# Batch 0 taken whole: both halves' attention from the lead-in's scores, and one output stage by seven block products

## The chip, the cores and the metric

The kernel runs on one core of a Trainium2 chip. The metric is the time of one execution on the device in microseconds. All numbers of the profile come from one profiled execution of the kernel.

## What is computed

For 4 batches of 8 heads, 768 positions and head size 64, each query attends to its neighbours closer than 16 positions and to 24 blocks of 32 keys, each represented by the maximum of its keys and the mean of its values (the block score has log 32 added). The result goes through a two-layer feed-forward network.

```python
k_sum = k.reshape(B, H, nb, block, D).max(axis=3)
v_sum = v.reshape(B, H, nb, block, D).mean(axis=3)
scores_l = np.where(mask_l, scale * q @ k.T, -1e9)      # mask_l: |i - j| < 16
scores_s = scale * q @ k_sum.T + np.log(block)
a = softmax(np.concatenate([scores_l, scores_s], axis=-1))
x = a @ np.concatenate([v, v_sum])                       # then [3072, 512]
h = x @ w_in                                             # 512 -> 2048
out = (h * sigmoid(1.702 * h)) @ w_out                   # 2048 -> 512
```

## The kernel before

The program is written as one long sequence; every engine executes its instructions in the order in which they are written, and each waits for the data that it needs. Work is placed beside other work by hand: small dictionaries (`plan0`, `plan1`, `plan`, `todo`) say which attention step is written after which slot of a matrix product.

A batch is 768 tokens in two halves of 384 (`HALF`), each of three tiles of 128. Heads go in four pairs `p`. The hidden layer has 16 tiles `nt` of 128; for a half and an `nt` it is four matmuls of 128x128 weights with 384 columns into PSUM (`ph`), then a gelu on ACT into `gT`.

**Two ways of attention.** In the lead-in, batch 0's first half goes by tiles of 128 queries against their own 128 keys (`s_own`), with small products for the 32 positions across a tile's edge (`s_edges`), the mask being added in PSUM by a matmul of a prepared `bias` (`s_bias`); `s_exp` takes the exponential. The block scores are products of their own (`b_turn`, `b_exp`), and values come from `v0n`, the batch's values as loaded, and `vs4`, its block sums (`v_sum`, `v_copy`), by `av_own`, `av_edges` and `av_blocks`; `v_norm` divides. All other half batches go by tiles of 64 queries against 128 rows that hold 64 own keys, two halos of 16 and the 24 block maxima with the rest (`kx`, filled by `tk` or `xk`, `rest_k`, `key_halos`, `key_rows`): `scores`, `mask`, `values`. For those the values' rows are laid out the same way in `vw`: `value_rows` has the halos copied by SP, sums blocks on PE (`vsum`), adds on DVE (`block_sums`) and has the sums' rows copied by SP (`sum_dmas`).

**Two ways of output.** Batch 0 takes its halves one after the other, and each half's output is 48 plain matmuls of 512 columns (`ff_out`, accumulated in `po`). Batches 1 to 3 take both halves together: from `gT`, DVE makes four sums `gs` (`g_sums`), from w_out once four sums `ws` (`w_sum`), and the output of both halves is made from seven block products (`product`, numbers 1 to 7, for each of three tiles `t`), each eight matmuls of 256 columns, accumulated in `poA`, `poB` and `poC`, in the order of `seq`.

**The order around the change.** Lead-in (scores and values of batch 0, first half, 874 to 983); hidden layer of that half (1061 to 1065); its output with batch 0's second half of attention beside it (`plan0`, 1072 to 1077); hidden layer of the second half with batch 1's keys and half its queries turned (`todo`, 1079 to 1087); its output with the rest of batch 1's attention beside it (`plan1`, 1090 to 1096); then the loop over batches 1 and 2 (1100), in which the hidden layer of both halves is followed by seven products with the next batch's whole attention beside them (`plan`), and batch 3 at the end with other means.

**Queues.** POOL issues the loads that cast from float32: k, q, v, w_in, w_out in the order of lines 876 to 895, then `load_batch`. SP issues the copies inside the chip's memory, the transposes by DMA (`xk`, `xq`, `dx`) and the output's stores.

**Buffers.** In PSUM after the lead-in, `pmm` has four banks (hidden tiles, `po`), `psb` two buffers of two banks (turns, scores and others).

Of the kernel before, what the change touches and what calls it, by code (L numbers as in the profile page):

```python
# [35 lines left out]
def kernel(  # L36
# [55 lines left out]
    def load_q0(g):  # L92
        if g == 0:
            qb2["early"] = castp2.tile([128, H, JH, D], BF16, name="qb", tag="qb")
        pool.dma_start(out=qb2["early"][:, 4 * g:4 * g + 4].rearrange("p h r d -> p h (r d)"),
                       in_=q[0, 4 * g:4 * g + 4, 0:HALF].rearrange("h (p r) d -> p h (r d)", r=JH))

    def load_q1(a):
        if a == 0:
            qb2["late"] = castp2.tile([128, H, JH, D], BF16, name="qb", tag="qb")  # L100
        pool.dma_start(out=qb2["late"][:, 2 * a:2 * a + 2].rearrange("p h r d -> p h (r d)"),
                       in_=q[0, 2 * a:2 * a + 2, HALF:S].rearrange("h (p r) d -> p h (r d)", r=JH))
# [29 lines left out]
    warm = lead.tile([128, 512], BF16, name="warm")  # L132
    band = [lead.tile([128, 128 + 2 * PAD], BF16, name=f"band{i}") for i in range(2)]
    NE = HALF + JH * 32
    bias = lead.tile([128, NE], BF16, name="bias")

# [13 lines left out]
    def bands():  # L150

        n = 128 + 2 * PAD
        src, step = wide, 1
        for dst in (band[0], band[1], band[0], band[1]):
            n -= step
            dve.tensor_tensor(out=dst[:, 0:n], in0=src[:, 0:n], in1=src[:, step:step + n], op=ALU.max)
            src, step = dst, 2 * step
        n -= 15
        dve.tensor_tensor(out=band[0][:, 0:n], in0=band[1][:, 0:n], in1=band[1][:, 15:15 + n], op=ALU.max)
        dve.tensor_scalar(out=band[1][:, 1:1 + n], in0=band[0][:, 0:n], scalar1=-FAR, scalar2=FAR,  # L160
                          op0=ALU.mult, op1=ALU.add)
        near, edge = (bias[:, a:b].rearrange("p (j c) -> p j c", j=JH) for a, b in ((0, HALF), (HALF, NE)))
        dve.memset(edge, FAR)
        for o, r, c in ((near, slice(0, 128), slice(34, 162)), (edge, slice(0, 32), slice(2, 34)),
                        (edge, slice(96, 128), slice(162, 194))):
            dve.tensor_copy(out=o[r], in_=band[1][r, c].unsqueeze(1)
                            .to_broadcast([r.stop - r.start, JH, c.stop - c.start]))

# [39 lines left out]
    w_out_sb = keep.tile([128, NT, d_model], F16, name="w_out_sb")  # L208

# [21 lines left out]
    def load_batch(b):  # L231
        if b == 3:
            pool.tensor_copy(out=gate2, in_=qTs[0][:, 0, 0:1])
        load_turned(k, b, kb2, "kb")
# [5 lines left out]
        if b < 3:  # L240
            load_turned(q, b, qb2, "qb", (1,) if b == 1 else (0, 1))
# [23 lines left out]
    def vsum(s):  # L265

        if s == 1 and not vs_ps[0]:
            ps = [pmm.tile([128, 512], F32, name="ps_vs", tag="mm") for e in range(2)]
        else:
            big = psb.tile([128, 1024], F32, name="ps_vs", tag="big")  # L270
            ps = [big[:, 0:512], big[:, 512:1024]]
# [44 lines left out]

    def vrows0():

        dve.tensor_copy(out=gate3[:, 1:2], in_=gate3[:, 0:1])
        v6 = vs4.rearrange("p (a g) c -> p g a c", g=4)  # L320
        o6 = vs.rearrange("p (a g) c -> p g a c", g=4)
        for g in range(4):
            dve.tensor_copy(out=o6[0:nb, g, :, 0:D], in_=v6[32 * g:32 * g + nb, g, :, 0:D])
        w5 = vw[0].rearrange("p (j e) h c -> p j e h c", e=2)
        sum_dmas(w5, JH)
# [53 lines left out]
    def k_late(p, eng):  # L379

        k4 = kx[p][0].rearrange("p (j e) c -> p j e c", e=2)
        for e in range(2):
            eng.tensor_copy(out=k4[:, JH - 1:NJ, e, e * 64:e * 64 + 64],
                            in_=kn[:, p, HALF - 128:S].rearrange("p (j e c) -> p j e c", e=2, c=64)[:, :, e])

    def q_turn(p):
# [3 lines left out]
        turn_plain(st["Q", p], qb2["early"][:, 2 * p:2 * p + 2])  # L390

    def q_copy(p, eng):
        copy(eng, qT[p][0][:, 0:HALF].rearrange("p (c r) -> p c r", r=JH),
# [8 lines left out]
    def q_late(p, eng):  # L402
        if p != 2:
            ps = psb.tile([128, 2048], BF16, name="ps_q", tag="big")
        else:
            ps = pmm.tile([128, 1024], BF16, name="ps_q", tag="mm")
        turn_plain(ps[:, 0:HALF], qb2["late"][:, 2 * p:2 * p + 2])
        copy(eng, qT[p][0][:, HALF:S].rearrange("p (c r) -> p c r", r=JH),
             ps[:, 0:HALF].rearrange("p (r c) -> p c r", r=JH))

    def s_bias(p):

        big = st["S", p] = pbig.tile([128, 1024], F32, name="ps_s", tag="big")
# [4 lines left out]
    def s_own(p):  # L418

        big = st["S", p]  # L420
        for j in range(JH):
            for h in range(2):
                r, o = slice(h * 64, h * 64 + 64), slice(j * 128, j * 128 + 128)
                pe.matmul(out=big[:, h * 512 + j * 128:h * 512 + j * 128 + 128], lhsT=kn[r, p, o],
                          rhs=qTs[0][r, p, o], start=False, stop=True, skip_group_check=True)

    def s_edges(p):

        big = st["S", p]
        for j in range(JH):  # L430
            for h in range(2):
                r, o = slice(h * 64, h * 64 + 64), h * 512 + HALF + j * 32
                pe.matmul(out=big[0:32, o:o + 32], lhsT=kn[r, p, j * 128 + 128:j * 128 + 160],
                          rhs=qTs[0][r, p, j * 128 + 96:j * 128 + 128], start=False, stop=True,
                          skip_group_check=True)
                if j:
                    pe.matmul(out=big[96:128, o:o + 32], lhsT=kn[r, p, j * 128 - 32:j * 128],
                              rhs=qTs[0][r, p, j * 128:j * 128 + 32], start=False, stop=True,
                              skip_group_check=True)

    def s_exp(p):
        a = a_sb[p] = lead.tile([128, 2, NE], BF16, name="a_sb", tag="a_sb", bufs=4)
        act.activation(out=a, in_=st["S", p].rearrange("p (h c) -> p h c", h=2)[:, :, 0:NE],
                       func=ACT.Exp, scale=scale)

    def b_turn(g):

        st["B", g] = pturn.tile([128, 512], F32, name="ps_b", tag="turn")
        for i in range(2):
            for h in range(2):  # L450
                o = i * 64 + h * 32
                r = slice(h * 64, h * 64 + 64)
                pe.matmul(out=st["B", g][o:o + 32, 0:HALF], lhsT=ks0[r, 2 * g + i],
                          rhs=qT[2 * g + i][0][r, 0:HALF], start=True, stop=True, skip_group_check=True)

    def b_exp(g):
        ab = st["ab", g] = lead.tile([128, HALF], BF16, name="ab", tag="ab", bufs=2)
        act.activation(out=ab, in_=st["B", g][:, 0:HALF], func=ACT.Exp, scale=scale)
# [32 lines left out]
    def av_own(p):  # L491

        if p < 2:
            st["V", p] = pturn.tile([128, 512], F32, name="ps_av", tag="turn")
        else:
            st["V", p] = pbig.tile([128, 1024], F32, name="ps_av", tag="big")[:, 0:512]
        pv, a = pv_of(p), a_sb[p]
        for hh in range(2):
            for j in range(JH):
                pe.matmul(out=pv[:, hh, j, 0:D + 1], lhsT=a[:, hh, j * 128:j * 128 + 128],  # L500
                          rhs=v0n[:, 2 * p + hh, j, 0:D + 1],
                          start=(hh == 0 and j == 0), stop=False, skip_group_check=True)

    def av_edges(p):
        pv = pv_of(p)
        for hh in range(2):
            ah = a_sb[p][:, hh]
            for j in range(JH):
                o = HALF + j * 32
                pe.matmul(out=pv[96:128, hh, j, 0:D + 1], lhsT=ah[0:32, o:o + 32],  # L510
                          rhs=v0n[0:32, 2 * p + hh, j + 1, 0:D + 1],
                          start=False, stop=False, skip_group_check=True)
                if j:
                    pe.matmul(out=pv[0:32, hh, j, 0:D + 1], lhsT=ah[96:128, o:o + 32],
                              rhs=v0n[96:128, 2 * p + hh, j - 1, 0:D + 1],
                              start=False, stop=False, skip_group_check=True)

    def av_blocks(p):
        for j in range(JH):
            pe.matmul(out=pv_of(p)[:, :, j, :],  # L520
                      lhsT=st["ab", p // 2][:, j * 128:(j + 1) * 128],
# [25 lines left out]
    def tq(p, s, eng):  # L547
        ps = pmm.tile([128, 1024], BF16, name="ps_t", tag="mm")[:, 0:S]
# [37 lines left out]
    def values(b, half, g):  # L586

        if b == 1:
            banks = [pmm.tile([128, 512], F32, name="ps_av", tag="mm") for i in range(2)]
        else:  # L590
            ps = psb.tile([128, 1024], F32, name="ps_av", tag="big")
            banks = [ps[:, i * 512:i * 512 + 512] for i in range(2)]
        pvs = []
        for i in range(2):
# [4 lines left out]
            for hh in range(2):  # L599
                for j in range(JH):  # L600
                    for e in range(2):
                        t = 2 * j + e
                        pe.matmul(out=pv[e * 64:e * 64 + 64, hh, j, :], lhsT=a[:, hh, t, :],
                                  rhs=vw[b % 2][:, half * TH + t, p + hh * NP if b else 2 * p + hh, 0:D + 1],
                                  start=True, stop=True, skip_group_check=True)
        x2[g] = attp.tile([128, 2, JH, 2, D], F16, name="x2", tag="x2", bufs=4)
        for i in range(2):
            norm(x2[g][:, :, :, i].rearrange("p h j d -> p j h d") if b else x2[g][:, i], pvs[i])
# [59 lines left out]
    def g_sums(j, eng=dve, which=(0, 1, 2, 3)):  # L668

        a1, a2 = gTb[:, j], gTb[:, j + NT // 2]  # L670
        l, r = slice(0, HALF), slice(HALF, S)
        for w in which:
            a, b_, op = {0: (a1[:, r], a2[:, r], ALU.add), 1: (gs[:, 0, j], a1[:, l], ALU.subtract),
                         2: (a1[:, l], a1[:, r], ALU.subtract), 3: (a2[:, l], gs[:, 1, j], ALU.subtract)}[w]
            eng.tensor_tensor(out=gs[:, w, j], in0=a, in1=b_, op=op)
# [84 lines left out]
    def product(b, t, what):  # L760
# [23 lines left out]
        def keep_it(name):  # L784
            if b + 1 == B and name == "s1":
# [3 lines left out]
            copy(dve if t == 0 and b + 1 < B else act, t_, po)  # L789
# [40 lines left out]

    N0 = 2
# [13 lines left out]

    po_now = {}

    def ff_out(u, ms, part):
        if part == 0:
# [382 lines left out]
```

## Time and profile before

| | us |
|---|---|
| median of 3 runs | 208.12 (207.81 to 208.46) |
| profiled execution | 207.35 |
| its span | 205.6 |
| hidden layer, first `ph` of the unbroken run | 21.18 |
| first output stage (`po`) | 31.26 to 45.97 |
| hidden layer of the second half | 45.97 to 58.38 |
| second output stage, with the block sums ahead of it | 58.38 to 76.18 |
| batch 1, hidden layer | 76.18 to 97.96 |
| batch 1, seven products | 97.96 to 120.52 |

| group (PE, matmul) | count | busy us |
|---|---|---|
| `ph`, 384 columns | 416 | 70.2 |
| `po`, 512 columns | 96 | 23.6 |
| `poA`, `poB`, `poC`, 256 columns | 504 | 65.4 |
| scores `ps_s`, 64 rows by 64 columns | 336 | 7.9 |
| values `ps_av` with `vw` | 336 | 7.0 |

The stages' times are the starts of pieces in the chain of work that ended last. Busy times of a group overlap with those of other groups, since matmuls are pipelined; the spacing of consecutive matmuls is read from the chain. The span leaves out 1.75 us of the profiled execution's time.

### The profile page before, as it was taken

How to read it: one execution, taken by the hardware profiler on the slowest of the kernel's cores; microseconds unless marked ns; L12 is line 12 of the kernel's file. 1: busy time of each engine (PE TensorE's matmuls, PEld its weight loads, DVE VectorE, ACT ScalarE, POOL GpSimd, SP SyncE). 2: the span in 40 equal slices, each digit the busy share in tenths (PEclk: the TensorE clock that was granted, in tenths of full speed). 3: DMA queues.
4: the chain of work that ended last, by engine and by line, in shares of the span. 5: the costliest groups of instructions: out<-in, count | busy, mean ns of one | idle time of the engine just before them, and what ended most of it. 6: DMA issues, size and time to landing. Idle time of an engine off the chain costs nothing.

```text
span 205.6 us, 5854 instructions
## 1 busy us (share of the span) xinstructions
PE 198.5 (97%) x2364; PEld 138.1 (67%) x2364; DVE 139.9 (68%) x388; ACT 123.7 (60%) x237; POOL 93.5 (45%) x145
## 2 busy tenths in 40 slices
PE   7889999999999999999999999999999999999992
PEld 7658564556754566565888875566888865668882
DVE  4767795594856793898757789896769546758221
ACT  2374975728885716677772446778670577983220
POOL 7976289645899585000977036000000019990000
PEclk9999999999999999999999999999999999999999
DMA  5999999999999999999999989999023640000223
GB/s 59 153 158 198 207 212 207 204 156 233 124 145 153 177 170 135 163 145 141 139 180 158 164 162 136 130 248 154 0 105 86 149 126 3 0 0 3 102 102 105
DMA packets 97131, 27.74 MB, mean 135 GB/s; under 512 B 86720, under 2 KB 94160, under 8 KB 97104
## 3 DMA queue, kind: packets, MB, share of 16 engines
q0 software_dynamic: 71472, 13.64, 90.7%
q1 hardware_dynamic: 25632, 13.74, 32.3%
q8 instruction: 18, 0.29, 0.7%
q14 instruction: 9, 0.07, 0.1%
HBM read 27.26 MB, written 6.29 MB: 163 GB/s over the span
## 4 chain that ended last, share of the span: by engine, by line
PE 90%; DMA 4%; POOL 3%; issue 1%; DVE 1%; ACT 0%; POOLq 0%; DVEq 0%
PE ph L28 33%; PE poA L28 16%; PE po L28 11%; PE poB L28 8%; PE ps_av L28 4%; DMA v0n<-in_v_dram 4%; PE poC L28 4%; PE phA L28 4%; PE ps_s L28 3%; PE ps_t L28 1%; POOL kb L28 1%; PE ps_x L28 1%; PE phB L28 1%; PE phC L28 1%; PE phE L28 1%; PE ps_vs L28 1%
## 5 line engine op out<-in xcount | busy, mean ns | idle before, releaser
L28 PE MATMUL ph<-xT,w_in_sb 128*128 128x384 f16 x416 | 70.2, 326 | 0.1
L28 PEld LDWEIGHTS <-w_in_sb 128*128 128x128 f16 x452 | 43.7, 98 | 27.8 <-issue 0.2
L28 ACT ACTIVATE gT<-ph 128x384 f16<-128x384 f32 x104 | 49.8, 491 | 18.5 <-PE ph L28 18.2
L28 PEld LDWEIGHTS <-gT 128*128 128x128 f16 x312 | 28.8, 98 | 11.0
L28 ACT ACTIVATE a_sb<-ps_s 128x768 bf16<-128x768 f32 (+1 forms) x32 | 25.0, 826 | 12.7 <-PE ps_s L28 12.7
L28 PEld LDWEIGHTS <-gs 128*128 128x128 f16 x288 | 27.7, 98 | 3.4
L28 POOL DMA_DIRECT2D vw<-in_v_dram x36 | 24.5, 694 | 12.0 <-DMA kb<-in_k_dram 6.3
L28 POOL TENSOR_TENSOR gs<-gT 128x384 f16<-128x384 f16 x9 | 8.2, 909 | 42.4 <-ACT gT L28 42.4
L28 PE MATMUL po<-w_out_sb,gT 128*128 128x512 f16 x96 | 23.6, 380 | 0.0
L28 DVE TENSOR_TENSOR a_sb<-a_sb,mk 128x768 bf16<-128x768 bf16 x28 | 14.9, 555 | 6.5 <-ACT a_sb L28 5.9
L28 PE MATMUL poA<-ws,gs 128*128 128x256 f16 x144 | 18.7, 273 | 0.0
L28 DVE TENSOR_TENSOR x<-ps_av,rc 128x384 f16<-128x384 f32 x32 | 17.8, 558 | 1.1
L28 DVE TENSOR_TENSOR gs<-gT 128x384 f16<-128x384 f16 (+1 forms) x34 | 13.4, 393 | 7.2 <-ACT gT L28 6.9
L28 POOL DMA_DIRECT2D qb<-in_q_dram x18 | 16.6, 936 | 1.9 <-DMA w_in_sb<-in_moe_w_in_dram 1.2
L28 POOL DMA_DIRECT2D kb<-in_k_dram x16 | 15.3, 970 | 1.2 <-POOLq L1216 0.8
L28 PEld LDWEIGHTS <-kx 64*128 64x128 bf16 (+1 forms) x372 | 9.4, 95 | 6.8 <-issue 4.4
L28 DVE TENSOR_REDUCE ks<-kx 128x24 bf16<-128x768 bf16 x12 | 11.4, 948 | 3.4 <-ACT kx L28 3.2
L28 ACT ACT_TABLE_LOAD x10 | 12.8, 1283 | 1.0 <-PEq L1216 0.8
L28 ACT ACTIVATE osb<-poA 128x256 f32<-128x256 f32 x9 | 3.5, 384 | 15.8 <-PE poA L28 15.8
L28 ACT ACTIVATE s<-poA 128x256 f32<-128x256 f32 x11 | 4.2, 385 | 11.2 <-PE poA L28 11.2
L28 PEld LDWEIGHTS <-a_sb 128*64 128x64 bf16 (+2 forms) x400 | 7.8, 108 | 2.8 <-issue 1.3
L28 PE MATMUL poA<-w_out_sb,gT 128*128 128x256 f16 x72 | 9.4, 273 | 0.0
(113 smaller groups left out, 281.4 us busy)
## 6 DMA issues: line engine op xcount, KB each, us to landing
out_dram<-osb SPq DMA_DIRECT2D x23, 256.0 KB, 3.7
kb<-in_k_dram POOLq DMA_DIRECT2D x16, 192.0 KB, 6.9
qb<-in_q_dram POOLq DMA_DIRECT2D x14, 192.0 KB, 9.2
vw<-in_v_dram POOLq DMA_DIRECT2D x36, 64.0 KB, 5.7
w_out_sb<-in_moe_w_out_dram POOLq DMA_DIRECT2D x4, 512.0 KB, 13.0
w_in_sb<-in_moe_w_in_dram POOLq DMA_DIRECT2D x3, 512.0 KB, 12.7
vw<-vs SPq DMA_DIRECT2D x6, 198.0 KB, 7.1
v0n<-in_v_dram POOLq DMA_DIRECT2D x4, 192.0 KB, 7.9
```

The source lines that it names most:

```text
L28: r = f(*a, **kw)
```

## The change

Batch 0 is handled as a whole, as batches 1 and 2 are in the output stage.

- Lead-in: the second half's queries are loaded ahead of the values, in two loads, and turned there; its scores are made there too by `s_own` and `s_edges` (no `s_bias`: the first product of a region starts it, and `near_mask` and `s_mask` multiply by a mask on DVE after the lead-in), with its block scores.
- Between: batch 0's second half's values (`values0`) are made between hidden tiles, from `v0n` and `vs4`. Its rows in `kx` and `vw` are no longer filled (`k_late`, `vrows0`, the halo copies and `clear`s of batch 0 in their former places go; `clear` remains for the batches to come). The `w_sum` and `g_sums` steps stand between hidden tiles. The order is a string of steps: l and r are a hidden tile of the first or second half, V `values0`, x the transposes of the second half's result, c `clear`, w `w_sum`, G and g `g_sums`.
- Output: the loop over batches starts at 0. Batch 0's output is made by seven products in the order `seq0`, with batch 1's whole attention beside them (`plan1`: k and t turn keys and queries, R is `value_rows`, s scores, m masks, v values, d transposes by DMA, x transposes by PE, K and V load batch 2's keys and values). Batch 2's queries are loaded in batch 1's hidden layer, and their transposes by DMA are written at its fifth step rather than its third.
- `vsum`, `tq` and `values` of batch 1 use `psb` rather than `pmm`; `tq` copies on ACT rather than DVE; in batch 0, ACT copies the first tile's kept sums.

The diff, cut to its core:

```diff
-    load_q0(0)
+    load_q0(0, 0, 4)
     load_k0(2, 3)
     load_k0(3, 4)
-    load_q0(1)
+    load_q0(0, 4, 4)
+    load_q0(1, 0, 4)
+    load_q0(1, 4, 4)
     for p in range(NP):
         load_v0(p)
...
-    load_w_out(0)
-    for a in range(NP):
-        load_q1(a)
-    for c in range(1, 3):
+    for c in (0, 2, 1):
         load_w_out(c)
...
-    k_max(2)
     s_bias(2)
     s_bias(3)
-    v_sum((0,))
     s_own(2)
-    s_own(3)
     s_edges(2)
     s_exp(2)
+    s_own(3)
     s_edges(3)
+    s_exp(3)
+    k_max(2)
+    q_turn(0, 1)
+    q_turn(1, 1)
+    q_copy(0, dve, 1)
+    q_copy(1, dve, 1)
+    q_turn(2, 1)
+    q_turn(3, 1)
+    q_copy(2, dve, 1)
+    q_copy(3, dve, 1)
+    k_max(3)
+    s_first(0)
+    s_own(0, 1)
+    s_edges(0, 1)
+    s_exp(0, 1)
...
+    v_sum((0,))
...
+    b_turn(1)
     v_sum((1,))
     v_copy((0, 1), dve)
-    k_max(3)
-    s_exp(3)
+    s_first(3)
+    s_own(3, 1)
+    s_edges(3, 1)
+    s_exp(3, 1)
+    b_exp(1)
     av_own(0)
...
+    b_turn(0, 1)
+    b_exp(0, 1)
     av_own(2)
...
+    b_turn(1, 1)
+    b_exp(1, 1)
     av_own(3)
...
+    near_mask()
+    for p in range(NP):
+        s_mask(p)
...
+    plan1 = {0: ['k0'], 1: ['k1'], 2: ['k2'], 3: ['k3', 'K', 'V'], 4: ['t0'], 5: ['t1', 'R'],
+             6: ['s00', 's01'], 7: ['m00', 'm01', 's10', 's11'], 8: ['t2', 'm10', 'm11'], 9: ['t3'],
+             10: ['s02', 's03'], 11: ['m02', 'm03', 'v00', 'd00', 's12'], 12: ['s13'],
+             13: ['v01', 'd01', 'm12'], 14: ['v10', 'd10', 'm13', 'g'], 16: ['v11'], 19: ['x11']}
...
+    def values0(g):
+        for p in (2 * g, 2 * g + 1):
+            av_own(p, 1)
+        for p in (2 * g, 2 * g + 1):
+            av_edges(p, 1)
+        for p in (2 * g, 2 * g + 1):
+            av_blocks(p, 1)
+        for p in (2 * g, 2 * g + 1):
+            v_norm(p)
...
+    run("c0 l2 l3 l4 l5 V0 l6 l7 V1 l8 x0 l9 l10 x1 l11")
+    run("c1 r0 w00 r8 G0 w10 r1 r9 G1 w20 l12 r2 r10 w30 l13 G2 r3 r11 l14 G3 w01 l15 r4 r12 G4 w11 "
+        "r5 r13 G5 w21 r6 r14 G6 w31 r7 r15 g7")
...
-    for i, (ms, part) in enumerate((ms, part) for part in range(4) for ms in range(JH)):
-        ff_out(0, ms, part)
-        beside0(i)
...
-    for i, (ms, part) in enumerate((ms, part) for ms in range(JH) for part in range(4)):
-        ff_out(1, ms, part)
-        beside(1, i)
...
-    for b in range(1, B - 1):
+    for b in range(0, B - 1):
...
-        for t, what in seq:
+        for t, what in seq if b else seq0:
             product(b, t, what)
             if i == 0:
                 g_sums(NT // 2 - 1, dve, (2, 3))
```

## The prediction, made before the changed kernel was run

> **What bounds the kernel now.** I read the page's busy table first, then the chain of work that ended last in order of time, then the timelines of PE, DVE and ACT in the lead-in, then the DMA landings.
>
> ```profile
> span 205.6 us, 5854 instructions
> PE 198.5 (97%) x2364; PEld 138.1 (67%) x2364; DVE 139.9 (68%) x388; ACT 123.7 (60%) x237; POOL 93.5 (45%) x145
> ```
>
> PE is the bound. The chain (start, length, what) shows where it begins to be, and prices every piece of PE work:
>
> ```profile
> 7.29 7.88 DMA v0n<-in_v_dram
> 15.21 0.52 PE ps_vt L28 x12
> 15.73 1.30 PE ps_av L28 x38
> ...
> 21.18 10.08 PE ph L28 x62
> 31.26 1.73 PE po L28 x8
> ...
> 34.91 0.57 DVE qT L28
> ...
> 39.99 0.88 PE ps_av L28 x48
> ...
> 58.91 0.46 PE ps_s L28 x24
> ...
> 67.98 0.50 PE ps_av L28 x24
> ...
> 76.18 1.30 PE ph L28 x8
> ...
> 98.41 0.98 PE poA L28 x8
> 99.39 0.87 PE poB L28 x8
> ```
>
> Until 15.2 PE waits for loads and copies; from 21.18 (first unbroken `ph`) to the end it hardly stops. So work taken off PE after 21.18 is worth its full time; work put into the lead-in costs only what its gaps do not hide. Batch 1's own hidden layer starts at 76.18; after it the program is the same but for one transpose, so I sum up to there. `po` x8 takes 1.73 (0.216 per 512 columns), `poB` x8 0.87 (0.109 per 256); the first eight after scores or values take 0.98, about 0.105 more, none more after a transpose.
>
> **The middle, 21.18 to 76.18.** Hidden layer of both halves: 10.08 + 10.40 = 20.48, unchanged.
> (1) Output: 96 x 0.2163 = 20.77 becomes 21 products of eight, 168 x 0.1092 = 18.34: -2.43.
> (2) Batch 0's second half beside the first output half: that stretch is 31.26 to 45.97 = 14.71, of which `po` 10.38 and two transpose groups 0.68 stay or move; the other 3.65 (query turns, scores, values, 0.57 waiting for DVE's qT, four switches) go: -3.65.
> (3) That half's values are now made as the lead-in makes them, in the hidden stage: two pairs cost 1.30 (the x38 line), four 2.60: +2.60.
> (4) Batch 1's attention: before 58.38 to 76.18 = 17.80 less `po` 10.38, plus six transposes in the hidden stage 2.04, plus one after 76.18 0.33: 9.79. After: eight turns 2.72, block sums 0.53, scores 3 x 0.46 + 2 x 0.28, values 4 x 0.50, one transpose 0.34, nine switches 0.95: 8.48. So -1.31; the gain is three x transposes given to SP's DMAs, and small waits.
> Sum -4.79. The other edits to loads (order of w_out, batch 2's keys and values issued from the plan) cost nothing: w_out is needed only from the sums at about 37 on, and batch 2's loads were issued at 60.67 before and can be there again.
>
> On (1) the row is the one number of weight: 288 matmuls of `gs`, 256 columns, at 0.109. [...] This trace has 216 and 109 ns, so its rows decide.
>
> **The lead-in.** Timelines of DVE and PE:
>
> ```profile
> 12.32 1.02 DVE L28 COPY qT<-ps_q 128x384 bf16<-128x384 bf16 x2 [0.41 <-PE ps_q L28]
> 13.26 0.94 DVE L28 TENSOR_REDUCE ks<-qT 128x24 bf16<-128x768 bf16 x1
> 15.57 1.01 PE L28 MATMUL ps_av<-v0n,a_sb 128*128 128x65 bf16 x32
> ```
>
> Two q loads (192 KB each) move ahead of v0n. The neighbours landed at 10.65 (last k) and 11.75 (last q), 1.1 apart, so v0n moves by 2.2: its second load, which released the chain at 15.2, lands at 17.4. w_in moves as much (landings 18.5 to 27.8 become 20.7 to 30.0), each part ahead of its first use, since the hidden stage moves by more. PE has the second half's turns and scores meanwhile. DVE sets the pace: the first-half copies end at 13.34, k_max 0.94 gives 14.2, four second-half copies at 0.49 give 16.15, k_max 17.1. Then PE: block scores 0.41, value sums 0.37, last scores 0.36 (0.76 for two pairs): the first `ps_av` starts at 18.25, not 15.57. From there to the unbroken `ph` it was 5.61; one more group of block scores adds 0.41, and the third pair's PSUM now waits for the first norm (1.23 after the blocks begin; PE is free 0.4 earlier). So 24.67: +3.5. Bounds: +2.2 (the loads alone), +5.4 (2.2 and all moved PE work, 0.93 + 1.44 + 0.82, unhidden). I take 3.5, since the DVE rows make a full chain.
>
> **New waits in the output stage.** It starts at 24.67 + 20.48 + 2.60 + 0.68 = 48.4. DVE carries clears, eight `ws` sums (0.64 apart) and the `gs` sums (1.29 per four) from 35.5: 1.2 + 5.1 + 9.0 + 0.7 gives 51.5; the first product that needs them is due at 52.1. Covered by 0.6. ACT's 16 copies and exps (0.7 to 0.8 each) fit between. Then the value rows: PE's sums end at 48.4 + 6 x 0.873 + 6 x 0.34 + 0.53 = 56.2. DVE still has four key maxima (0.95) and two adds (0.42) from 52.2, until 56.8, and block sums take 1.5: 58.3. They hold a PSUM buffer that the second score needs at about 57.4: wait 0.9, and PE is strict in order, so all products stand behind it. SP then copies the rows:
>
> ```profile
> 60.62 1.75 SPq L28 DMA_DIRECT2D vw<-vs  x2
> DMA to landing us min/median/max: 3.0/7.4/9.8
> ```
>
> (SP's timeline; the landings of `vs`'s copies.) Before, the later copy landed at 66.9, 6.3 after the block sums ended; so now 64.6. The first values are due at 63.9 without waits, 64.8 with the 0.9: just covered. The last score waits for the first values' norms, 0.25, and small ones 0.2. Sum +1.4, bounds 0 (DVE or the loads earlier; 0.77 MB of stores that lay beside batch 1's loads are gone) and +4.9 (a landing of 9.8 instead of 6.3). I take the rows of the same copy.
>
> **Sum.** -4.79 + 3.5 + 1.4 = +0.1 on the span of 205.6: 205.7. The profiled execution took 207.35 (1.75 around its span); the median of the runs is 208.12. I put +0.1 on the median: 208.2. A difference within 0.3%, 0.62 us, counts as none.
>
> **The rivals.**
> A, the forecast: a level trade, -1.0 to +1.0 (207.1 to 209.2). Chance 0.45: faster 0.11, same 0.25, slower 0.09.
> B, faster: the waits are hidden (batch 1's loads land earlier without the stores, DVE keeps its lead) and the lead-in grows by 3.0: -4.79 + 3.0 + 0.3 = -1.5, 206.6. For it: `vw` landed at 57.0 behind those stores. Against: DVE at 56.8 is no load. Chance 0.22.
> C, slower: the value rows come last. From `R` at slot 5 to the first values at slot 11 there are some 8 us; before there were 9.1 (58.91 to 67.98), with 1.1 to spare. The copies share the DMA engines with batch 2's key loads, issued at the same time. It decides as soon as the landing is over 6.5 after the block sums; at 9.8 the wait is 3.3: up to 211.5, and with half that wait 209.9. Chance 0.20. [...]
> D, slower: the lead-in loses what I hide (ACT has eight 0.97 exps, not four): +4.8, 209.5. Chance 0.10.
> E: the products save nothing here, weight loads (98 ns) holding 0.109 up to 0.124: +2.4, 210.6. Against: 504 such matmuls in later stages. Chance 0.03.
>
> **Numbers.** Faster 0.11 + 0.22 = 0.33; same 0.25; slower 0.09 + 0.20 + 0.10 + 0.03 = 0.42. The range 206.3 to 210.6 holds A, B, D, E and the lower half of C.
>
> **What would show it.** Unbroken `ph` from 24.2 to 25.2; no waits before the output stage at 48 to 49; the first product eight at 0.87; batch 1's hidden layer beginning at 75.5 to 77.5. Wrong if the `ph` start is past 25.5 (D), if PE idles over 1.5 before the first `ps_av` of `vw` (C), or if the waits in the stage sum to under 0.5 (B).

## The result, and the profile after

The changed kernel takes 214.71 us (median of 6 runs, 213.21 to 215.97) against 207.78 us for the kernel before in runs beside it: a ratio of 1.033, interval 1.028 to 1.038. The forecast was 208.2, at most 210.6. The profiled execution took 213.99, its span 212.2. A ratio, here and below, leaves out runs over 1.5% above the fastest of the same kernel; a median takes all.

Three lines of the page after:

```profile
span 212.2 us, 6082 instructions
PE 200.1 (94%) x2478; PEld 148.2 (70%) x2478; DVE 143.5 (68%) x392; ACT 126.5 (60%) x244; POOL 91.8 (43%) x144
...
PEclk9999699999999999999999999999999999999999
```

PE does 114 more matmuls in only 1.6 us more of busy time, but its share falls from 97% to 94%: it waits, and in one slice of the span (the fifth, 21.2 to 26.5 us) it is granted a lower clock. The chain of work that ended last (start, length, what) says where:

```profile
19.72 1.47 issue
...
27.56 3.58 PE ph L28 x22
...
37.67 13.65 PE ph L28 x84
51.32 0.87 PE poA L28 x8
...
61.61 7.74 DMA vw<-vs
69.48 0.54 PE ps_av L28 x23
...
71.30 0.42 DVE osb L28
...
82.96 5.20 PE ph L28 x32
```

Three of these lines are no PE work, in places where the chain before had none: 1.47 of "issue" (PE waits for nothing that the profile names), a copy between buffers of 7.74, and DVE's `osb`, after which the chain runs through DVE's masks and norms until 78.65, with one group of values between. By stage, from the two chains:

| stage | before | after | change predicted | change measured |
|---|---|---|---|---|
| up to the unbroken `ph` | 21.18 | 27.56 | +3.5 | +6.38 |
| from there to batch 1's hidden layer | 55.00 | 55.40 | -3.06 | +0.40 |
| of it: hidden layer with the second half's values | | 23.76 | 23.76 in all | as predicted |
| of it: the output stage | | 31.64 | 28.2 in all | 3.4 more |
| the rest of the span | 129.42 | 129.24 | -0.33 | -0.18 |

So 2.9 us more than forecast were lost in the lead-in and 3.4 in the output stage, and the arithmetic on products and hidden tiles held. PE's waits up to 90 us, summed by what ended them:

```profile
PE ps_av L28 <- DMA vw<-vs: 1.6, 1, 1.6
PE ps_av L28 <- DVE x L28: 1.6, 1, 1.6
PE ps_av L28 <- issue: 1.5, 1, 1.5
...
PE ps_s L28 <- DVE vs L28: 0.4, 1, 0.4
```

The first is the value rows that come late (rival C), the third is the lead-in's gap, the fourth the block sums, predicted at 0.9. The second was in no part of the prediction. With one of 0.3 before the fourth values, the waits in the output stage sum to 3.9 against the 1.4 of the forecast; the other 0.9 of the 3.4 stands in no wait that this list names. DVE's timeline leads to the cause of the second:

```profile
66.32 0.42 DVE L28 TENSOR_TENSOR osb<-poC,qT 128x256 f32<-128x256 f32 x1 [1.47 <-PE poC L28]
71.30 0.42 DVE L28 TENSOR_TENSOR osb<-poA,s 128x256 f32<-128x256 f32 x1 [4.55 <-PE poB L28]
```

DVE stands still for 4.55 us ahead of an `osb`, and masks and norms queue behind it until 74.06. The profile names PE's `poB`, but this `osb` reads `poA`, whose matmuls end at 67.72. `osb` is an output tile; its pool holds three. SP's timeline shows what is out:

```profile
60.98 1.23 SPq L28 DMA_DIRECT2D vw<-vs  x2
62.26 3.06 SPq L28 DMA_DIRECT2D out_dram<-osb  x2
```

In the order `seq0` the `osb` at 71.30 opens the fourth output tile, and needs the buffer of a store issued in the second line. That store landed at 71.2, 8.9 us after its issue.

### The profile page after: what moved, and what is told of

Read it like the earlier page. It is cut to its first block, busy times and chain, and to the rows that moved or that the text cites. A ratio compares the mean times of both kernels' runs of the same rounds, so it can differ in the third digit from the quotient of the medians.

```text
span 212.2 us, 6082 instructions
## 1 busy us (share of the span) xinstructions
PE 200.1 (94%) x2478; PEld 148.2 (70%) x2478; DVE 143.5 (68%) x392; ACT 126.5 (60%) x244; POOL 91.8 (43%) x144
## 4 chain that ended last, share of the span: by engine, by line
PE 85%; DMA 6%; DVE 4%; issue 2%; ACT 1%; POOL 0%; SPq 0%; DVEq 0%; POOLq 0%
PE ph L28 32%; PE poA L28 18%; PE poB L28 9%; PE ps_av L28 5%; PE poC L28 5%; PE ps_s L28 4%; DMA vw<-vs 4%; PE phA L28 4%; DMA kb<-in_k_dram 2%; DVE x L28 2%; PE phB L28 1%; PE phC L28 1%; DVE a_sb L28 1%; PE ps_t L28 1%; PE phE L28 1%
## 5 line engine op out<-in xcount | busy, mean ns | idle before, releaser
L28 PEld LDWEIGHTS <-gs 128*128 128x128 f16 x384 | 36.5, 98 | 4.8 <-issue 0.3
L28 PEld LDWEIGHTS <-gT 128*128 128x128 f16 x288 | 27.2, 98 | 3.9
L28 PE MATMUL poA<-ws,gs 128*128 128x256 f16 x192 | 24.9, 273 | 0.1
L28 DVE TENSOR_TENSOR gs<-gT 128x384 f16<-128x384 f16 (+1 forms) x50 | 18.1, 380 | 9.7 <-ACT gT L28 9.3
L28 DVE TENSOR_TENSOR a_sb<-a_sb,mk 128x768 bf16<-128x768 bf16 x24 | 12.7, 553 | 3.6 <-ACT a_sb L28 3.2
L28 ACT ACTIVATE s<-poA 128x256 f32<-128x256 f32 x16 | 6.2, 386 | 11.7 <-PE poA L28 11.1
L28 PE MATMUL poA<-w_out_sb,gT 128*128 128x256 f16 x96 | 12.5, 273 | 0.0
L28 PE MATMUL poB<-ws,gs 128*128 128x256 f16 x96 | 12.5, 273 | 0.0
L28 PE MATMUL poA<-ws,gT 128*128 128x256 f16 x96 | 12.5, 273 | 0.0
L28 PE MATMUL poB<-w_out_sb,gs 128*128 128x256 f16 x96 | 12.5, 273 | 0.0
```

Source lines behind the costliest of these rows:

```text
L28: r = f(*a, **kw)
```

## What the lead-in's gap is

In the windows of the lead-in (stretch, length, busy times of PE, PEld, DVE, ACT and POOL, then the granted clock, the DMA share, 1.23 to 1.64 here, and GB/s) the gap and the clock stand one behind the other:

```profile
17.50:20.00 2.50, 2.22 (x63) 1.74 (x60) 0.42 (x1) 2.20 (x4) 1.83 (x3) 1.00 1.64 192
20.00:22.50 2.50, 1.31 (x27) 1.01 (x26) 0.34 (x2) 0.53 (x2) 2.06 (x9) 0.89 1.31 204
22.50:25.00 2.50, 2.50 (x39) 1.80 (x35) 1.82 (x5) 0.63 (x2) 2.14 (x10) 0.50 1.26 212
25.00:27.50 2.50, 2.43 (x38) 1.64 (x35) 0.76 (x3) 1.91 (x6) 2.36 (x6) 0.93 1.23 202
```

The gap in PE's timeline:

```profile
21.19 0.25 PE L28 MATMUL ps_av<-v0n,a_sb 32*32 32x65 bf16 x5 [1.47 <-issue]
```

No engine holds PE here: ACT's exponentials end at 20.25, and ACT and DVE then stand idle until PE has gone on. What may be missing is instructions. The page lists their loads as a DMA queue of its own (packets, MB, share):

```profile
q8 instruction: 19, 0.31, 0.6%
```

0.31 MB in 19 packets is 16 KB each. If they are PE's, one packet stands for some 130 matmuls: 19 for 2478 here, and 18 for 2364 on the page of before. In the changed kernel the gap stands right after the 351st matmul. (351 is no multiple of 128; the places found below, 223, 351 and 479, are 128 apart, and why the first falls where it does was not followed up.) Whether it is a matter of count, and not of what the 352nd matmul does, the runs below decide. The theory, then: PE's program comes in blocks of 128 matmuls; a block is asked for when the one before is begun (an assumption, no trace shows the request), takes some 6 us to come in during the lead-in (6.31 here, from 14.88 to 21.19), and PE starves when it gets through 128 matmuls sooner. The changed lead-in has a denser run of small matmuls: the block that begins with the 224th is worked off in 4.65 us (14.88 to 19.53, by the matmuls' own times). Before, the one between the same counts took 6.8.

The trace also has the packets of that queue one by one. In the changed kernel one begins at 18.90 and takes 0.89, and PE goes on at 21.19, 1.40 after its end. In every run, each gap at such a place (twelve in ten runs) ends 1.3 to 1.7 us after the end of a 16 KB packet of this queue, whatever the work behind the gap.

## Experiments

Each run's time stands beside runs of the kernel before on the same chip; the ratio is to that.

**1. Fewer and wider warm-up matmuls.** The opening warm-up as 9 matmuls of 512 columns, not 36 of 128.

```diff
-    idle(36)
+    idle(9, 512)
```

> The changed kernel; the lead-in's first 36 idle matmuls of 128 columns become 9 of 512 (the same PE time, 54 PE instructions fewer). Theory 1 (PE runs out of fetched instructions in the lead-in: its 1.47 us idle at 19.72 has no releaser, ends when a 16 KB instruction fetch that began at 18.9 is in, and the half clock from 21.95 to 25.36 follows from that idle time): the gap is under 0.3, the granted clock stays at 1.00, the unbroken hidden layer starts at 24.5 to 25 instead of 27.4, the time falls by 2.5 to 3. Rival (the lead-in of the change simply leaves PE too idle, and the gap is a throttle): the half clock and the start at 27 stay, under 0.5 gained.

Measured: 214.37, ratio 1.029 (1.022 to 1.035). No gain, where 2.5 to 3 were expected, and the half clock stayed (0.50 to 0.57 in the windows from 22.50 to 30.00), as the rival has it. But the gap moved, 27 matmuls further into the work, and a smaller one of 0.58 turned up right after the 223rd:

```profile
16.55 0.39 PE L28 MATMUL ps_s<-qT,qT 64*128 64x32 bf16 x10 [0.58 <-issue]
...
22.75 0.91 PE L28 MATMUL ps_av<-v0n,a_sb 128*128 128x65 bf16 x16 [1.64 <-issue]
```

The two stand 128 matmuls apart. Shifting the blocks against the work did not make the work less dense.

**2. A fourth output buffer.** Tile 1's first-half and second-half outputs go to a free part of `qTs[0]`.

```diff
-                now[t, o] = outp.tile([128, d_model], F32, name="osb", tag="osb")
+                if b == 0 and t == 1:
+                    c0 = N1 + (0 if o == "o1" else d_model)
+                    now[t, o] = qTs[0].rearrange("p a b -> p (a b)").bitcast(F32)[:, c0:c0 + d_model]
+                else:
+                    now[t, o] = outp.tile([128, d_model], F32, name="osb", tag="osb")
```

> The changed kernel; batch 0's two output buffers of the second tile stand in the idle space of batch 0's queries, so that the pool of three is not used up. Theory 2 (DVE's 4.55 us before the add at 71.3 is the wait for an output buffer whose store takes 8.9 us, and masks and norms stand behind it): that wait is gone, the waits of 1.56 and 0.34 before the second and fourth values go, the wait of 1.6 for the value rows stays; 1.5 to 2 us gained. Rival (all follows from the late value rows): DVE then waits for the norms instead, under 0.5 gained.

Measured: 212.98, ratio 1.025 (1.022 to 1.028): 1.7 less. DVE's 4.55 and PE's 1.6 are gone, and the wait for the value rows grows to 2.0. The buffer is a cause, and of the size expected.

**3. Batch 2's loads written later.** `plan1`'s K and V from slot 3 to slot 12.

> The changed kernel; batch 2's keys and values are issued after slot 12 instead of slot 3. Theory 3 (the value rows' copies and the stores share the DMA engines with these loads): the later copy lands in 4 to 5 us instead of 7.7, the store in 4 to 5 instead of 8.9, both waits are gone and the output stage is 3 to 3.5 us shorter; batch 1's block sums may then wait for values that come later, which takes back some of it. Rival (copies of many small pieces are slow by themselves): landings stay at 7 to 9 and nothing is gained.

Measured: 214.83 (four runs from 211.71 to 215.08), ratio 1.026 (1.017 to 1.036). The edit did nothing to what it aimed at: POOL had nothing to wait for and issued the key loads at 58.77 all the same. So it does not test the theory on the value rows. By chance its profiled execution, the fastest of the four, had a gap of only 0.75 after the 351st matmul and a full clock (1.00); there the unbroken `ph` stands at 25.87 in PE's timeline, against 27.40.

**4. The kernel before with 36 more warm-up matmuls.** The same columns, narrower.

```diff
-    idle(36)
+    idle(72, 64)
```

> The kernel before; its first 36 idle matmuls of 128 columns become 72 of 64 (the same columns, 72 PE instructions more). Theory 1: the kernel before now runs out of instructions as well, with an idle time on PE at 17 to 20 us that has no releaser and perhaps a half clock after it: 1 to 4 us slower. Rival (no limit by instructions): the same time within 0.3%.

Measured: 209.01, ratio 1.004 (1.001 to 1.007). The kernel before, which has no gap, gets one, and it stands after the 351st matmul:

```profile
20.49 0.34 PE L28 MATMUL ps_av<-v0n,a_sb 32*32 32x65 bf16 x10 [1.07 <-issue]
```

**5. The same with 128 more** (28 columns each), one whole block.

```diff
-    idle(36)
+    idle(164, 28)
```

> The kernel before with its opening warm-up of 36 matmuls of 128 columns as 164 of 28 columns: 128 matmuls more, one whole instruction block, nearly the same columns. Theory (blocks of 128 matmuls): the blocks are cut at the same places of the work as before, so there is no gap, unlike with 36 more: 207.2 to 208.4, ratio 1.000. Rival (more small matmuls cost time by themselves, 36 of them cost 0.9): a gap or 3 us more in the warm-up, 209 to 211.

Measured: 207.45, ratio 0.999 (0.996 to 1.002), no gap. 36 more small matmuls cost 1 us and 128 more nothing: what counts is where the blocks are cut, as the theory says. A cost of small matmuls as such, the rival, does not explain it.

**6. The changed kernel with the fourth buffer and 92 more warm-up matmuls** (`idle(128, 36)`).

> The changed kernel with the fourth output buffer of tile 1 (212.98 by itself) and the opening warm-up of 36 matmuls of 128 columns as 128 of 36 columns: the same columns, 92 matmuls more, so the 351st matmul is the one that was the 259th and the 479th the one that was the 387th. Theory (PE gets its instructions in blocks of 128 matmuls, a block arrives some 6 us after the one before it is begun): the gap with no releaser leaves its old place and stands right after the 351st or the 479th matmul, or in two parts after both, 1.0 to 1.8 in sum; if both parts are under 1.1, the clock stays full and the time is 211.2 to 212.3; otherwise 212.3 to 213.3. Rival (something in the work at the first edge values holds PE): the gap stays there, 1.5, and the time is 213.

Measured: 212.38, ratio 1.020 (1.015 to 1.025), against 212.98 in experiment 2 and within the 212.3 to 213.3 expected. The gap left its old place and stands right after the 479th matmul, 351 + 128:

```profile
22.98 0.28 PE L28 MATMUL ps_av<-v0n,a_sb 32*32 32x65 bf16 x7 [1.33 <-issue]
```

Over the runs with a gap after the 351st or 479th matmul, the time from entering a block to having the next one is 5.7 to 6.5 us (block entered at 14.71, next one there at 20.49 in experiment 4; 16.79 and 22.98 here), whatever the work in it.

**7. Forty matmuls fewer in the lead-in.** The second half's edge scores as one 96-column matmul per head; its edge scores are not the reference's.

```diff
-                    if not after and u:
+                    if u:
+                        if not after and j == 0:
+                            pe.matmul(out=big[:, h * 512 + HALF:h * 512 + NE], lhsT=kn[r, p, k0:k0 + 128],
+                                      rhs=qTs[0][r, p, k0:k0 + JH * 32], start=True, stop=True,
+                                      skip_group_check=True)
+                    elif not after and u:
```

> The changed kernel; the second half's edge scores are one 96-column matmul a head instead of six of 32 (their values are not the edge scores then), which takes 40 matmuls, 80 PE instructions, out of the lead-in and only some 0.5 us of PE time. Theory 1 in its new form (each 128 matmuls are one 16 KB block of instructions; a block is asked for when PE enters the one before it and comes 5.8 to 6.3 us later under the loads of the lead-in; the changed kernel runs through matmuls 223 to 351 in 4.65 us): PE's gap without a releaser is 0.3 us at most, no half clock, unbroken hidden layer at 24.3 to 25.3 instead of 27.4, 2.5 to 3.5 us gained. Rival (the half clock comes from the lead-in's idle PE as such): gap and half clock stay somewhere, under 1 us gained.

Measured: 210.84, ratio 1.013 (1.008 to 1.017): 3.9 less. There is no gap in the lead-in (the list of waits has one of 0.3 by "issue", but at 71.15, in the output stage), the clock is full (1.00 from 17.50 to 27.50), and PE's timeline has the unbroken `ph` 2.36 earlier:

```profile
25.04 3.74 PE L28 MATMUL ph<-xT,w_in_sb 128*128 128x384 f16 x22
```

The other 1.5 came from the output stage: there is no wait for the value rows. SP issues their copies 0.8 ahead of POOL's first load of batch 2's keys, and they land in 4.6 (median); in the changed kernel the same copies follow those loads by 1.7 and take 6.2. Experiment 7, then the changed kernel:

```profile
58.62 1.24 SPq L28 DMA_DIRECT2D vw<-vs  x2
59.42 4.04 POOL L28 DMA_DIRECT2D kb<-in_k_dram  x4
...
60.98 1.23 SPq L28 DMA_DIRECT2D vw<-vs  x2
59.26 4.04 POOL L28 DMA_DIRECT2D kb<-in_k_dram  x4
```

The time that the lead-in loses puts the copies behind the loads. The profiled execution gained only 2.6: batch 1's hidden layer took 1.2 longer in it, with short waits for the transposes by DMA of the result (0.4) and of batch 2's queries (0.6).

**8 to 10. The loads held back until the rows have landed.** POOL reads the last rows of `vw` before it issues batch 2's loads; alone, with the fourth buffer, and with that and experiment 7's edit.

```diff
-    3: ['k3', 'K', 'V'] ... 5: ['t1', 'R'],
+    3: ['k3'] ... 5: ['t1', 'R', 'W', 'K', 'V'],
+            elif what == "W":
+                pool.tensor_copy(out=gate2[64:96], in_=vw[1][64:96, NQ - 2, 0, 0:1])
+                pool.tensor_copy(out=gate2[0:32], in_=vw[1][0:32, NQ - 1, 0, 0:1])
```

> The changed kernel; batch 2's keys and values are written after R at slot 5, behind two small POOL copies that read the last value rows, so POOL can only issue them when the rows have landed (the late-loads run moved them in the program, but POOL had nothing to wait for and issued them at the same 59 us). Theory 3 (rows and stores share the DMA engines with these loads): the later rows' copy lands in 4 to 5 us instead of 7.3 to 8.2, the 1.2 to 2.2 us wait before the first values is gone, the store of the first output lands early enough that DVE's wait shrinks as well: 2 to 3.5 us gained against the changed kernel. Rival (these copies are slow by themselves): they still take over 7 us, nothing gained.

> The gated loads together with the two extra output buffers. Theory: both waits of the output stage are gone, PE's waits in it sum to under 1.5 us and the stage takes 28 to 28.5 us instead of 31.6: 3 to 3.5 us gained against the changed kernel. If the buffers add nothing to the gate, the store's landing was the only cause.

> All three: fewer edge matmuls, gated loads, two more output buffers (the edge scores of the second half are left out here too). If the three causes are separate and complete, the gains add up to 6 to 7 us: 207.5 to 209, within 0.5% of the kernel before. If the sum is much less, the same time was counted twice or another wait stands behind them.

Measured: 217.49 (1.048, 1.043 to 1.052), 216.44 (1.041, 1.037 to 1.045) and 213.36 (1.027, 1.022 to 1.032). In the first the copies were issued at 61.22, POOL found the rows landed at 64.09 and 65.91, and the first values waited for nothing: the copies are slow because of the loads. Yet the kernel got 2.8 slower, where 2 to 3.5 less were expected, and the other two runs missed their 3 to 3.5 less and 207.5 to 209 as well. The loads now meet the transposes by DMA of batch 1's result, which take 6.9, 8.1 and 9.7 (4.9, 3.6 and 4.8 in the changed kernel), and its chain shows the price:

```profile
75.94 9.74 DMA xT<-x
85.68 0.05 issue
85.73 5.30 PE ph L28 x16
```

PE waits 2.9 for that transpose and falls to half clock a second time (0.50 from 86.00 to 90.00; 5.30 for 16 matmuls, where experiment 11 below has 2.77). Holding loads back moves the collision to the next transfer. In the third, which has experiment 7's edit, gaps of 0.50 and 0.57 stand after the 223rd and the 351st matmul all the same, with the clock at 1.00: the few edges leave little margin.

**11. Both repairs that paid:** experiment 7's edit and the fourth buffer.

> The changed kernel with both repairs that have paid: 40 fewer matmuls in the lead-in (the second half's edge scores are one 96-column matmul per head; its edge scores are not the reference's) and the fourth output buffer of tile 1 in a free part of qTs[0]. Theory (instruction fetch in the lead-in plus the output buffer): the first took 3.9 off and left DVE a 1.0 wait for the buffer, so 210.8 - 1.0 = 209.8, range 209.2 to 210.4, clock 1.00, no wait of DVE for a store in the stage at 60 to 75. Rival (the two losses are separate, 3.9 and 1.7): 209.1. Rival (the buffer's wait in the run with few edges was covered): 210.8.

Measured: 211.34, ratio 1.017 (1.012 to 1.022), not the 209.8 expected. DVE's wait is gone, and the chain has a new one in its place:

```profile
72.74 9.43 DMA xT<-x
82.22 2.77 PE ph L28 x16
```

PE idles 2.1 before that `ph`. This is the transpose by DMA again, issued earlier now and 9.43 us under way. A second wait of 1.3 comes before batch 1's first product, at 102.57; the profile names DVE's `gs`, and what held DVE was not followed up:

```profile
PE ph L28 <- DMA xT<-x: 2.1, 1, 2.1
PE ps_s L28 <- DVE gs L28: 1.3, 1, 1.3
```

**12. The same with batch 1's result turned by PE,** as the kernel before did it.

```diff
-    11: ['m02', 'm03', 'v00', 'd00', 's12'], ... 13: ['v01', 'd01', 'm12'], 14: ['v10', 'd10', 'm13', 'g'],
+    11: ['m02', 'm03', 'v00', 's12'], ... 13: ['v01', 'x00', 'm12'], 14: ['v10', 'm13', 'g'], 15: ['x01'],
-    16: ['v11'], 19: ['x11']
+    16: ['v11'], 17: ['x10'], 19: ['x11']
```

> The run with few edge scores and the fourth output buffer, and batch 1's result turned by PE (three groups of six transposes, 0.34 each, one DVE copy each) as the kernel before did, not by SP's DMA transposes; its edge scores are not the reference's. Theory (in that run the repairs' gain ended in the wait of 2.1 for the DMA transpose of the result, 9.4 us from issue to landing): PE gains 2.1 and pays 3 x 0.34 = 1.0: 211.3 - 1.1 = 210.2, range 209.4 to 210.9, no wait of ph for xT at the end of the stage. Rival (the wait turns up again at the DVE copies or at the next transposes by DMA, of batch 2's keys): 211.3 or more.

Measured: 208.73, ratio 1.004 (1.000 to 1.008): 2.6 less than experiment 11, more than the 1.1 expected, since both of that run's waits are gone (2.1 + 1.3 less the 1.0 for the transposes is 2.4), and level with the kernel before to within what the interval can tell. Its chain and PE's waits up to 90 us:

```profile
24.86 3.58 PE ph L28 x22
...
34.97 13.65 PE ph L28 x84
48.62 0.87 PE poA L28 x8
```

```profile
PE ps_s L28 <- DVE vs L28: 0.6, 1, 0.6
PE ps_av L28 <- DVE x L28: 0.4, 1, 0.4
PE ps_q L28 <- DMA qb<-in_q_dram: 0.3, 1, 0.3
```

The unbroken `ph` at 24.86 (forecast 24.67), batch 1's hidden layer at 77.91: a stage of 29.29, which is 28.27 beside the 1.02 for the three transposes on PE (forecast 28.2).

**13. The full kernel, all scores as wanted, with the fourth buffer and the result turned by PE.**

> The changed kernel, all scores as the reference wants them, with the fourth output buffer (212.98 by itself) and batch 1's result turned by PE. Theory: there the first DMA transpose's wait was hidden behind the wait of 2.0 for the value rows, so PE's 1.0 for the transposes is paid and little is gained: 213.0 to 214.0. Rival (the DMA transposes are what keeps the stores and loads behind them late): under 212.5.

Measured: 213.58, ratio 1.022 (1.013 to 1.032), against 212.98 in experiment 2. With the lead-in's gap (1.68 here) and the wait for the value rows (1.7) in place, there is nothing to gain from it, as expected.

## Why the prediction was wrong, step by step

**The middle, right.** Eight product matmuls take 0.87, as the row of `gs` had it. The hidden layer with the second half's values took 23.76, the predicted figure. So the seven products' gain of 2.43 and the 3.65 of the second half's separate stage were had, as far as these rows show; other losses cover them.

**The lead-in, the step that failed first.** The prediction followed loads, DVE and PE's work. The first `ps_av` was to start at 18.25 and did at 18.79, so that chain was nearly right. What it put at nothing is the supply of PE with instructions. The gap of 1.47 and about 1.3 of half clock behind it (6.12 from the third `ps_vt` group to the unbroken `ph`, against 4.84 in experiment 7) make up some 2.7 of the 2.9 us by which `ph` came later than 24.67. The bound of +5.4 was passed, since it was a sum of work and loads alone. Experiments 4, 5 and 6 and the packets of the instruction queue show the cause. Experiment 7 shows its price, 2.36, some of which is the work of its 40 matmuls (0.5 by the estimate ahead of it). The half clock's share shows in other runs too: in experiments 6 and 13 the one execution with a mean granted clock of 1.000 is the fastest of its four (211.08 against 212.32 to 212.68, and 211.64 against 213.14 to 214.30). The prediction's own sign, a `ph` past 25.5, came up, but not by its rival D: ACT's exponentials had ended before the gap was over.

**The value rows, mis-sized.** The landing was put 6.3 after the block sums, as before; it came 8.4 after (60.95 to 69.34). Rival C had its mechanism and its threshold right, 6.5, and its sign, over 1.5 of idle PE before the first values, came up at 1.6. That rival was given 0.20 with the copies and the loads "issued at the same time", as they were before (60.62 and 60.67), without asking which would go first now. That is what decides. The later copy took 4.6 when the copies went 0.8 ahead of the loads (experiment 7), 5.9 and 5.6 when both went together (11 and 12), none of them with a wait; 7.3 when they went 0.7 behind (experiment 3), with a wait of 1.2; 7.7 when 1.7 behind, with 1.6. With the lead-in on its forecast, the rows would probably have been in time, as in experiments 7 and 12.

**The output buffers, missed.** The prediction counted the stores that no longer lie beside batch 1's loads as a relief. It did not follow the stores of this stage, nor count output tiles against the pool's three buffers in the new order. Price alone: 1.7.

**The transposes by DMA, of the wrong sign.** Giving three of them to SP was entered as a gain of about 1 us of PE work. With the other losses away it is a loss: experiments 11 and 12 differ by 2.6 in the other direction, of which 2.1 is the wait for the transpose itself. In the changed kernel itself it doesn't show (experiment 13), probably since earlier waits give the transposes time.

**The forecast's sum.** The three losses taken away leave 208.73. That is 0.5 above the forecast's 208.2, and 1.0 above was due with the transposes on PE; but experiment 7's edit also takes the work of 40 small matmuls away, so the agreement is not exact evidence. No version that computes everything and keeps PE supplied in the lead-in was found; the kernel before remains the fastest.

## What to carry to other kernels

Count instructions as well as microseconds: here PE's gaps stood 128 matmuls apart, and the next 128 could go on 5.7 to 6.5 us after the ones before were begun, in a stretch with some 200 GB/s of other loads. The changed lead-in got through 128 in 4.65; PE then stood still for 1.47, and 3.4 at a granted clock of 0.50 followed. When a stage is made shorter by moving attention and stores into it, follow every transfer to the buffer that it frees and ask which load is ahead of it; here the same copies took a third longer (6.2 against 4.6), and the last transpose twice as long (9.7 against 4.8), when they came behind a batch's loads.

## What the runs showed of the hardware

- By the places of the gaps and the packets, loads of its program held PE up. In the lead-in, at some 200 GB/s of casting loads, the next 16 KB of PE's program were there 5.7 to 6.5 us after the block before it was begun: in the changed kernel the packet begins 4.0 after that, takes 0.9, and PE goes on 1.4 after its end. PE idled 0.50 to 1.96 us at a block's edge (twelve gaps in ten runs), and with the count of warm-up matmuls alone a gap came (36 more, experiment 4), stayed away (128 more, experiment 5) and moved by 128 (92 more, experiment 6). That the other loads are what delays the packet is likely, but no run separates it.
- The lower clock isn't a matter of a gap's length alone. Gaps of 1.33 to 1.96 in the lead-in were followed by a granted clock of 0.50 (for 3.4 or 6.8 us), gaps of 0.5 to 1.07 and a wait of 1.24 in experiment 11 were not; but in the output stage waits of 1.6 and 2.1 left it at 1.00, and waits of 2.5 and 2.9 (experiments 9 and 8) did not. Why some pauses are followed by the lower clock and others aren't stays open.
- Copies, stores and transposes by DMA took up to 2.7 times as long beside POOL's casting loads: the rows' copies took 3.4 (median) with the loads held back (experiment 8), 4.6 ahead of the loads (experiment 7) and 6.2 behind them (the changed kernel), a store 8.9 there against a median of 3.6 over that kernel, a transpose by DMA 9.7 (experiment 8) against a median of 3.6 in the changed kernel.
